# Attention with a gated output: the output projection over pairs of token tiles, and other places for the weight loads

## The chip, the cores and the metric

The kernel runs on one core of a Trainium2 chip. The metric is the device time of one execution in microseconds. Three runs of the kernel before took 563.62, 563.86 and 562.90 us; their median is 563.62 us. The execution that was profiled took 563.68 us, and its trace spans 561.8 us from the first instruction to the last. Times of day in this document ("at 212.36 us") count from the start of that span.

## What is computed

The input x has 2048 tokens of width D = 512. The reference, cut to what matters:

```python
xn = layernorm(x)
# A: attention over the last W = 512 rows of a cache; 32 query heads, 8 key/value heads, Dh = 128
q = (xn @ wq)                      # 2048 x 4096, split into 32 heads
p = softmax(q @ k.T * Dh ** -0.5)  # per head: 2048 x 512
s = concat_heads(p @ v) @ wo       # wo is 4096 x 512
# B: a dense MLP of width F = 1792 on the same xn
g = silu(silu(xn @ w1) @ w2)
out = x + s * g
```

Everything is bfloat16 in memory; matmuls accumulate in float32.

## The kernel before, in words

**Tiling.** The tokens are cut into NBLK = 4 blocks of BLK = 512, a block into BLKT = 4 token tiles of P = 128. The main loop (L454) runs over NSTEP = 128 *steps*: step s is head h = s mod 32 of block b = s // 32. All five engines' orders are written out by hand inside `manual_schedule` (L329): on each engine instructions stand in the order in which the Python code emits them, and an engine takes its own in order.

**One step** emits, between them, parts of four heads (L464 to L489):

- the four scores of head s, one token tile each (`score`, L224), each followed by an exponential on ScalarE that also sums the row (L227);
- `normalise` (L235): a reciprocal (L237) and one multiply per token tile (L239) on VectorE. Tiles 0 and 1 of step s are normalised in step s, tiles 2 and 3 at the head of step s + 1;
- `flip(s - 1)` (L245): one DMA transpose of the normalised probabilities p_all into pT, 512 KB from on-chip memory to on-chip memory, issued from SyncE (SP);
- the q projection of head s + 2, four matmuls and a copy (L205, L214);
- the PV product of head s − LAG, LAG = 3, four matmuls (L256) and a copy to `oT` (L261), the head's output transposed: features on partitions, the block's 512 tokens along the row. So pT of step s is wanted in step s + 3.

**Filler.** `pump(n)` puts n single matmuls of other work between these. In block 0 (steps 0 to 31) the filler is the MLP of blocks 1 to 3 (block 0's MLP is done ahead of the loop). From step 32 on it is the output projection of the block before, 128 matmuls per block, four to a step: two after the third score and two after the fourth. I call them *units*, numbered 0 to 127 within a block; unit u falls in the block's step u // 4.

**The output projection** is made by `out_units(b)` (L285). For token tile j the 32 heads add into one PSUM tile `s_ps` (L294), tag "f" with two buffers: `oT` of the head, the tile's 128 columns, is the stationary operand, and the head's 128 x 512 slice of wo the moving one. At head 16 GpSimd issues the load of the tile's x (`x_e`, L303). After head 31 VectorE multiplies with the gate (`sg`, L307) and adds x (L308), and the result is stored (L311), by GpSimd, or by SP for the last block. The order is tile 0 with heads 0 to 31, then tile 1, and so on. The last block's 160 matmuls (tile 3 in two halves) have no step left to hide in and run after the loop (L504 to L512), among the last three PV products.

**Buffers.** `oT` has OT_BUFS = 53 buffers used in turn. `x_e` has two (tags pair4 and pair5), `sg` two (pair2, pair3); these tags belonged to the MLP before.

**wo** is 4 MB in all and takes the room of the MLP's weights when these are done. It comes in pieces, each one DMA on SP: `wo_plan` (L442) gives for a step the pieces (first head, number of heads; 128 KB per head) that are issued at the step's end (L501, L280). The first four pieces, heads 0 to 13, are issued at the ends of steps 27 to 30; the others, heads 14 to 31, at the ends of steps 32 to 36. A unit needs the piece that holds its head.

**Order on the queues.** SP's queue in this stretch holds the flips and the wo pieces alone[...]. GpSimd's queue holds the x_e loads and the stores of blocks 0 to 2.

Of the kernel before, what the change touches and what calls it, by code (L numbers as in the profile page):

```python
# [9 lines left out]
P = 128  # L10
ALU = mybir.AluOpType
ACT = mybir.ActivationFunctionType
ENG = mybir.EngineType
BF16 = mybir.dt.bfloat16
FP32 = mybir.dt.float32

LAG = 3
OT_BUFS = 53
PS_BUFS = {"sc": 4, "q": 1, "o": 1, "f": 2}


# [1 line left out]
def kernel(  # L23
# [12 lines left out]
    nc = tc.nc  # L36
    _B, SQ, D = A_x.shape
    NTOK = _B * SQ
    _, HKV, SK, DH = A_k_cache.shape
    HQ = A_wq.shape[1] // DH  # L40
# [6 lines left out]
    BLKT = 4  # L47
# [6 lines left out]
    x2 = A_x.flatten_outer_dims()  # L54
# [5 lines left out]
    reg = ctx.enter_context(tc.tile_pool(name="reg", bufs=1))  # L60
    work = ctx.enter_context(tc.tile_pool(name="work", bufs=2))
    ps = ctx.enter_context(tc.tile_pool(name="ps", bufs=1, space=bass.MemoryType.PSUM))
# [10 lines left out]
    g_sb = {}  # L73
# [175 lines left out]
    def pv_units(s):  # L249
# [3 lines left out]
        def mm(kc):  # L253
# [5 lines left out]
            if kc == NKC - 1:  # L259
                oT[s] = work.tile([P, BLK], BF16, name="oT", bufs=OT_BUFS)  # L260
                nc.vector.tensor_copy(oT[s], cur["ps"])  # L261
# [6 lines left out]
    def wo_of(h):  # L268
        for lo, n, t in wo_t:
            if lo <= h < lo + n:  # L270
                return t[:, h - lo, :]
        raise KeyError(h)
# [4 lines left out]
    def load_wo(h0, n):  # L277
        for lo, m, t in wo_t:
            if lo <= h0 < lo + m:
# [2 lines left out]
                    A_wo[ds(h0 * DH, n * DH), :].rearrange("(h p) n -> p h n", p=P),  # L282
                )

    def out_units(b):  # L285
        units = []
        cur = {}
        last = b == NBLK - 1

        def mm(j, h, lo, n):  # L290
            t = b * BLKT + j
            if h == 0:
                cur["ps"] = ps.tile([P, n], FP32, name="s_ps", tag="f", bufs=2)
            nc.tensor.matmul(  # L294
                cur["ps"],
                oT[b * HQ + h][:, j * P : (j + 1) * P],
                wo_of(h)[:, lo : lo + n],
                start=(h == 0),
                stop=(h == HQ - 1),
            )  # L300
            if h == HQ // 2 and lo == 0:
                cur["x"] = reg.tile([P, D], BF16, name="x_e", tag=f"pair{4 + j % 2}")
                nc.gpsimd.dma_start(cur["x"], x2[ds(t * P, P), :])  # L303
            if h == HQ - 1:
                xe = cur["x"][:, lo : lo + n]
                sg = reg.tile([P, n], FP32, name="sg", tag=f"pair{2 + (j + lo // 256) % 2}")
                nc.vector.tensor_tensor(out=sg, in0=cur["ps"], in1=g_sb[b][:, j, lo : lo + n], op=ALU.mult)  # L307
                nc.vector.scalar_tensor_tensor(  # L308
                    out=xe, in0=sg, scalar=0.25, in1=xe, op0=ALU.mult, op1=ALU.add
                )  # L310
                (nc.sync if last else nc.gpsimd).dma_start(out2[ds(t * P, P), lo : lo + n], xe)  # L311

        for j in range(BLKT):
            parts = [(0, D // 2), (D // 2, D // 2)] if last and j == BLKT - 1 else [(0, D)]
            for lo, n in parts:
                for h in range(HQ):
                    units.append(lambda j=j, h=h, lo=lo, n=n: mm(j, h, lo, n))
        return units

    w1v = B_w1.rearrange("(c p) f -> p c f", p=P)  # L320
    w2v = B_w2.rearrange("(c p) d -> p c d", p=P)
# [7 lines left out]
    with tc.manual_schedule(engines={ENG.PE, ENG.Activation, ENG.DVE, ENG.SP, ENG.Pool}):  # L329
# [71 lines left out]
        for i, u in enumerate(hs[NEARLY * ND :]):  # L401
            u()
            f, c = divmod(i + NEARLY * ND, ND)
            if c == ND - 1 and f in (5, 7, 9, 11):
                stats(1, (f - 5) // 2)
        for i, u in enumerate(os_):
# [6 lines left out]
            if i % 4 == 3 and 1 <= i // 4 <= 2 * BLKT:  # L413
                b, j = divmod(i // 4 - 1, BLKT)
# [20 lines left out]
        def pump(n):  # L435
# [8 lines left out]
            HQ - 4: [(4, 3)],  # L444
            HQ - 3: [(7, 4)],
            HQ - 2: [(11, 3)],
            HQ: [(14, 4)],
            HQ + 1: [(18, 3)],
            HQ + 2: [(21, 4)],
            HQ + 3: [(25, 3)],  # L450
            HQ + 4: [(28, 2), (30, 2)],
        }
        wo_first = False
        for s in range(NSTEP):  # L454
            b, h = divmod(s, HQ)
            if b >= 1 and h == 0:
                assert done >= n_mlp or b > 1
                fill += out_units(b - 1)
            n = (h + 1) * n_mlp // HQ - done if b == 0 else 4
# [41 lines left out]
            for args in wo_plan.get(s, []):  # L501
                load_wo(*args)

        fill += out_units(NBLK - 1)  # L504
        s = NSTEP
        normalise(s - 1, 2, 3)
# [36 lines left out]
```

The softmax here doesn't subtract the row's maximum and nothing guards it: scores larger than these inputs give would overflow.

## Time and profile before

| What | Value |
|---|---|
| median of three runs | 563.62 us |
| span of the profiled run | 561.8 us |
| TensorE busy | 549.1 us, 2576 matmuls |
| VectorE busy | 439.7 us |
| ScalarE busy | 385.5 us |
| mean DMA throughput | 160 GB/s |
| DMA transposes pT<-p_all | 128, median 3.7 us from issue to landing |
| granted TensorE clock | 1.00 |

How to read it: TensorE is busy for all but 12.7 us of the span. The page names each group of instructions by line, engine and operation, with out<-in by the program's tile names; "PE" is TensorE's matmuls, "PEld" its weight loads, "SPq" the queue of SyncE, which issues DMAs. In a timeline a row is: start, duration (both us), engine, line, operation, tiles, count, and in brackets the idle time of the engine ahead of it with what ended it. A list of stretches gives for each its length, then busy time of PE, PEld, DVE, ACT and POOL with instruction counts in parentheses, then the granted clock, the mean busy share of the 16 DMA engines, and GB/s; the share counts overlapping packets, so it can exceed 1. In the list of waits a row is: who waited for whom, total us, number of waits, longest.

### The profile page before, as it was taken

What the parts mean: (1) busy time and instruction counts of PE and PEld (TensorE: products, weight loads), DVE (VectorE), ACT (ScalarE), POOL (GpSimd) and SP (SyncE); (2) the same over time, 40 slices, a digit from 0 to 9 for tenths busy, and PEclk for the clock granted to TensorE, in tenths of its full rate; (3) what the DMA queues carried; (4) which work ended last, traced back from release to release, by engine and by line L of the source; (5) the groups of instructions that cost most, each with busy time, mean ns of one, the idle gap of its engine ahead of it and who ended that gap; (6) DMA issues with size and microseconds to landing.
All of it is one profiled execution on the core that took longest, in us unless ns stands there. A gap on an engine that the chain in (4) does not pass through costs nothing.

```text
span 561.8 us, 8230 instructions
## 1 busy us (share of the span) xinstructions
PE 549.1 (98%) x2576; PEld 250.8 (45%) x2576; DVE 439.7 (78%) x1185; ACT 385.5 (69%) x1110; POOL 16.5 (3%) x35
## 2 busy tenths in 40 slices
PE   8989999999999997999999999999999999999997
PEld 4434444444444443444444444444444444444345
DVE  5978877976887685888888888888888888888622
ACT  4758757766776675777777777777777777777400
POOL 0000000000000000000000000000000000000100
PEclk9999999999999999999999999999999999999999
DMA  9638596885747899768676767676868685868701
GB/s 301 177 85 169 115 200 145 158 194 127 169 109 183 161 221 231 169 156 169 151 169 152 168 151 169 151 175 147 182 143 185 137 192 130 191 138 181 179 28 29
DMA packets 297467, 89.67 MB, mean 160 GB/s; under 512 B 282320, under 2 KB 296528, under 8 KB 297424
## 3 DMA queue, kind: packets, MB, share of 16 engines
q1 hardware_dynamic: 295280, 84.83, 67.8%
q0 software_dynamic: 1344, 3.67, 2.8%
q10 hardware_dynamic: 800, 0.66, 0.4%
q8 instruction: 20, 0.33, 0.3%
q14 instruction: 23, 0.19, 0.1%
HBM read 17.30 MB, written 2.10 MB: 35 GB/s over the span
## 4 chain that ended last, share of the span: by engine, by line
PE 87%; DVE 6%; DMA 4%; ACT 2%; issue 1%; ACTq 0%; SPq 0%
PE o_ps L256 19%; PE q_ps L205 19%; PE sc_ps L224 19%; PE s_ps L294 18%; PE oB_ps L172 7%; PE h_ps L138 6%; DMA pT<-p_all 4%; DVE st L104 2%; ACT th L149 1%; DMA x_116<-in_A_x_dram 1%; DVE mv L105 1%; ACT p_all L227 0%; DVE p_all L239 0%; DVE x_122 L115 0%; DVE hT_2_479 L150 0%
## 5 line engine op out<-in xcount | busy, mean ns | idle before, releaser
L227 ACT ACTIVATE p_all<-sc_ps 128x512 bf16<-128x512 f32 x512 | 304.9, 597 | 109.9 <-PE sc_ps L224 100.6
L239 DVE TENSOR_SCALAR p_all<-p_all,rden 128x512 bf16<-128x512 bf16 x512 | 157.8, 350 | 9.1
L261 DVE CAST oT<-o_ps 128x512 bf16<-128x512 f32 x128 | 88.2, 689 | 51.7 <-PE o_ps L256 51.6
L227 ACT ACTIVATION_READ_ACCUMULATOR p_all<-sc_ps 128x1 f32 x512 | 100.6, 196 | 0.0
L214 DVE CAST qT<-q_ps 128x512 bf16<-128x512 f32 x128 | 88.0, 687 | 2.8 <-PE q_ps L205 2.8
L294 PEld LDWEIGHTS <-oT 128*128 128x128 bf16 x544 | 53.2, 98 | 57.6
L224 PEld LDWEIGHTS <-qT 128*128 128x128 bf16 x512 | 50.1, 98 | 61.6 <-issue 1.8
L237 DVE RECIPROCAL rden<-den 128x2 f32<-128x2 f32 x256 | 40.6, 159 | 14.5 <-ACT p_all L227 14.5
L149 ACT ACTIVATE th<-h_ps 128x512 bf16<-128x512 f32 x56 | 33.4, 598 | 10.6 <-PE h_ps L138 8.4
L294 PE MATMUL s_ps<-wo_2010,oT 128*128 128x512 bf16 (+1 forms) x119 | 33.0, 366 | 0.0
L294 PE MATMUL s_ps<-wo_2317,oT 128*128 128x512 bf16 (+1 forms) x119 | 33.0, 366 | 0.0
L294 PE MATMUL s_ps<-wo_2318,oT 128*128 128x512 bf16 (+1 forms) x119 | 32.8, 367 | 0.0
L294 PE MATMUL s_ps<-wo_2011,oT 128*128 128x512 bf16 (+1 forms) x119 | 32.8, 367 | 0.0
L224 PE MATMUL sc_ps<-kT_89,qT 128*128 128x512 bf16 x64 | 24.3, 379 | 0.0
L224 PE MATMUL sc_ps<-kT_91,qT 128*128 128x512 bf16 x64 | 24.3, 379 | 0.0
L224 PE MATMUL sc_ps<-kT_86,qT 128*128 128x512 bf16 x64 | 24.3, 379 | 0.0
L224 PE MATMUL sc_ps<-kT_87,qT 128*128 128x512 bf16 x64 | 24.3, 379 | 0.0
L224 PE MATMUL sc_ps<-kT_90,qT 128*128 128x512 bf16 x64 | 24.3, 379 | 0.0
L224 PE MATMUL sc_ps<-kT_88,qT 128*128 128x512 bf16 x64 | 24.3, 379 | 0.0
L224 PE MATMUL sc_ps<-kT_85,qT 128*128 128x512 bf16 x64 | 24.3, 379 | 0.0
L224 PE MATMUL sc_ps<-kT_92,qT 128*128 128x512 bf16 x64 | 23.9, 379 | 0.0
L256 PE MATMUL o_ps<-pT,v_94 128*128 128x512 bf16 x64 | 17.1, 379 | 1.9 <-DMA pT<-p_all 1.9
(198 smaller groups left out, 700.0 us busy)
## 6 DMA issues: line engine op xcount, KB each, us to landing
pT<-p_all SPq DMA_TRANSPOSE x128, 3.7
x_e<-in_A_x_dram POOLq DMA_DIRECT2D x16, 128.0 KB, 2.9
out_dram<-x_e POOLq DMA_DIRECT2D x12, 128.0 KB, 2.2
w_1_106<-in_B_w_dram SPq DMA_DIRECT2D x1, 896.0 KB, 8.1
w_0_107<-in_B_w_dram SPq DMA_DIRECT2D x1, 896.0 KB, 11.2
w_1_108<-in_B_w_dram SPq DMA_DIRECT2D x1, 896.0 KB, 13.2
w_0_105<-in_B_w_dram SPq DMA_DIRECT2D x1, 512.0 KB, 5.6
x_122<-in_A_x_dram SPq DMA_DIRECT2D x1, 512.0 KB, 9.1
```

The costliest lines, as they stand in the source:

```text
L138: nc.tensor.matmul(h_ps[:, lo : lo + n], w1_sb[f // FH][:, c, (f % FH) * P : (f % FH + 1) * P], xnT[b][:, c, lo : lo + n], start=(c == 0), ...
L149: nc.scalar.activation(th, h_ps, ACT.Tanh, scale=0.5)
L172: nc.tensor.matmul(cur["ps"], hT[b][f // 2][:, f % 2, j * P : (j + 1) * P], w2_sb[f // FH][:, f % FH, :], start=(f == 0), stop=(f == NFC - 1),
L205: nc.tensor.matmul(cur["ps"], wq_sb[h // REP][:, c, (h % REP) * DH : (h % REP + 1) * DH], xnT[b][:, c, :], start=(c == 0), stop=(c == ND - 1),
L214: nc.vector.tensor_copy(qT[s], cur["ps"])
L224: nc.tensor.matmul(sc, qT[s][:, j * P : (j + 1) * P], kT[h // REP], start=True, stop=True)
L227: nc.scalar.activation(p_all[s][:, :, j, :], sc.rearrange("p (kc q) -> p kc q", q=P), ACT.Exp, scale=INV_SQRT_DH, accum_out=den[s][:, j : ...
L237: nc.vector.reciprocal(rden, den[s][:, j0 : j1 + 1])
L239: nc.vector.tensor_scalar_mul(p_all[s][:, :, j, :], p_all[s][:, :, j, :], rden[:, j - j0 : j - j0 + 1])
L256: nc.tensor.matmul(cur["ps"], v_sb[h // REP][:, kc, :], pT[s][:, kc, :], start=(kc == 0), stop=(kc == NKC - 1))
L261: nc.vector.tensor_copy(oT[s], cur["ps"])
L294: nc.tensor.matmul(cur["ps"], oT[b * HQ + h][:, j * P : (j + 1) * P], wo_of(h)[:, lo : lo + n], start=(h == 0), stop=(h == HQ - 1),)
```

## The change

Three things are edited.

1. The order of the units of blocks 0 to 2. A new function `out_order` walks through two token tiles j0 and j0 + 1 at a time: two heads of j0, then two heads of j0 + 1, eight heads (LEAD) behind. The last block keeps its order. Tile j0 now starts at unit 0 and ends at unit 53, tile j0 + 1 starts at unit 10 and ends at unit 63; the second pair likewise from 64 on (64 to 117 and 74 to 127). The matmuls of a block are the same 128. Two accumulations are now open at once, one in each of the two "f" buffers, so the dictionary that held one PSUM tile and one x_e holds one for each j.
2. The wo pieces for heads 14 to 31 go from the ends of steps 32 to 36 to the ends of steps 33, 35, 37, 39 and 41. In the new order, head 14 is first wanted by unit 20 (step 37), head 18 by unit 28 (step 39), head 21 by unit 33 (step 40), head 25 by unit 41 (step 42) and head 28 by unit 48 (step 44). Before, they were wanted in steps 35, 36, 37, 38 and 39.
3. `oT` gets 48 buffers instead of 53. A head's output is last read by the fourth tile, which starts at unit 74 instead of 96.

On GpSimd's queue the order load, store, load, store of a block's x_e and results becomes load, load, store, store for each pair.

```diff
-OT_BUFS = 53
+OT_BUFS = 48
+LEAD = 8
...
+    def out_order(last):
+        order = []
+        for j0 in range(0, BLKT, 2):
+            if last:
+                for j in (j0, j0 + 1):
+                    parts = [(0, D // 2), (D // 2, D // 2)] if j == BLKT - 1 else [(0, D)]
+                    order += [(j, h, lo, n) for lo, n in parts for h in range(HQ)]
+                continue
+            for h in range(0, HQ + LEAD, 2):
+                if h < HQ:
+                    order += [(j0, h, 0, D), (j0, h + 1, 0, D)]
+                if h >= LEAD:
+                    order += [(j0 + 1, h - LEAD, 0, D), (j0 + 1, h - LEAD + 1, 0, D)]
+        return order
+
     def out_units(b):
-        units = []
-        cur = {}
+        acc = {}
+        xes = {}
         last = b == NBLK - 1
 
         def mm(j, h, lo, n):
             t = b * BLKT + j
             if h == 0:
-                cur["ps"] = ps.tile([P, n], FP32, name="s_ps", tag="f", bufs=2)
+                acc[j] = ps.tile([P, n], FP32, name="s_ps", tag="f", bufs=2)
             nc.tensor.matmul(
-                cur["ps"],
+                acc[j],
...
             if h == HQ // 2 and lo == 0:
-                cur["x"] = reg.tile([P, D], BF16, name="x_e", tag=f"pair{4 + j % 2}")
-                nc.gpsimd.dma_start(cur["x"], x2[ds(t * P, P), :])
+                xes[j] = reg.tile([P, D], BF16, name="x_e", tag=f"pair{4 + j % 2}")
+                nc.gpsimd.dma_start(xes[j], x2[ds(t * P, P), :])
...
-        for j in range(BLKT):
-            parts = [(0, D // 2), (D // 2, D // 2)] if last and j == BLKT - 1 else [(0, D)]
-            for lo, n in parts:
-                for h in range(HQ):
-                    units.append(lambda j=j, h=h, lo=lo, n=n: mm(j, h, lo, n))
-        return units
+        return [lambda a=a: mm(*a) for a in out_order(last)]
...
-            HQ: [(14, 4)],
-            HQ + 1: [(18, 3)],
-            HQ + 2: [(21, 4)],
-            HQ + 3: [(25, 3)],
-            HQ + 4: [(28, 2), (30, 2)],
+            HQ + 1: [(14, 4)],
+            HQ + 3: [(18, 3)],
+            HQ + 5: [(21, 4)],
+            HQ + 7: [(25, 3)],
+            HQ + 9: [(28, 2), (30, 2)],
```

More of the change, by code (lines that the diff above doesn't have):

```diff
@@ L301, in mm @@
             if h == HQ // 2 and lo == 0:
-                cur["x"] = reg.tile([P, D], BF16, name="x_e", tag=f"pair{4 + j % 2}")
-                nc.gpsimd.dma_start(cur["x"], x2[ds(t * P, P), :])
+                xes[j] = reg.tile([P, D], BF16, name="x_e", tag=f"pair{4 + j % 2}")
+                nc.gpsimd.dma_start(xes[j], x2[ds(t * P, P), :])
             if h == HQ - 1:
-                xe = cur["x"][:, lo : lo + n]
+                xe = xes[j][:, lo : lo + n]
                 sg = reg.tile([P, n], FP32, name="sg", tag=f"pair{2 + (j + lo // 256) % 2}")
-                nc.vector.tensor_tensor(out=sg, in0=cur["ps"], in1=g_sb[b][:, j, lo : lo + n], op=ALU.mult)
+                nc.vector.tensor_tensor(out=sg, in0=acc[j], in1=g_sb[b][:, j, lo : lo + n], op=ALU.mult)
                 nc.vector.scalar_tensor_tensor(
```

## The prediction

> **What bounds the kernel now.** The page's first part comes first: is there an engine with nothing left to give?
>
> ```profile
> span 561.8 us, 8230 instructions
> ...
> PE 549.1 (98%) x2576; PEld 250.8 (45%) x2576; DVE 439.7 (78%) x1185; ACT 385.5 (69%) x1110; POOL 16.5 (3%) x35
> ```
>
> TensorE is busy for 549.1 of 561.8 us, and the change neither adds nor removes a matmul. Only the 12.7 us between them can be won, and each of the gaps has to be found. The list of PE's waits has one large entry, the chain of waits places it, and PE's timeline between 195 and 230 us shows it:
>
> ```profile
> PE o_ps L256 <- DMA pT<-p_all: 4.2, 5, 1.9
> ```
>
> ```profile
> 205.74 16.30 DMA pT<-p_all x3
> ```
>
> ```profile
> 207.52 1.03 PE L256 MATMUL o_ps<-pT,v_93 128*128 128x512 bf16 x4
> ...
> 212.36 1.04 PE L256 MATMUL o_ps<-pT,v_93 128*128 128x512 bf16 x4 [1.22 <-DMA pT<-p_all]
> ...
> 216.56 1.04 PE L256 MATMUL o_ps<-pT,v_93 128*128 128x512 bf16 x4 [0.57 <-DMA pT<-p_all]
> ...
> 222.08 1.04 PE L256 MATMUL o_ps<-pT,v_94 128*128 128x512 bf16 x4 [1.89 <-DMA pT<-p_all]
> ...
> 225.54 1.03 PE L256 MATMUL o_ps<-pT,v_94 128*128 128x512 bf16 x4
> ```
>
> Each row is the PV product (`o_ps`) of one step. A step after block 0 has 16 matmuls and takes 3.455 us wherever nothing waits (from 315.44 to 343.07 us, eight of them take 27.63). From 207.52 to 225.54 us four steps take 18.02 instead of 13.82: **4.2 us are lost here**, all of it waiting for the transposed probabilities (pT) of steps 34, 35 and 36. (The brackets add to 3.7; a matmul's modelled end laps over the next start, so I count from row to row.) Outside this place and the last steps the trace has PV rows 3.455 us apart to the end of block 3, but for a single 0.1 us at 260 us.
>
> Why they are late is in SyncE's own timeline and in the DMA share of a busy and a quiet stretch of equal length:
>
> ```profile
> 201.13 0.58 SPq L280 DMA_DIRECT2D wo_2317<-in_A_wo_dram  x1
> 201.87 3.08 SPq L245 DMA_TRANSPOSE pT<-p_all  x1
> 204.99 0.58 SPq L280 DMA_DIRECT2D wo_2318<-in_A_wo_dram  x1
> 205.74 4.58 SPq L245 DMA_TRANSPOSE pT<-p_all  x1
> 210.37 0.58 SPq L280 DMA_DIRECT2D wo_2318<-in_A_wo_dram  x1
> ```
>
> ```profile
> 195.00:222.00 27.00, 23.39 (x107) 10.12 (x105) 19.93 (x57) 17.11 (x52) 0.00 (x0) 1.00 1.03 212
> 315.00:342.00 27.00, 27.00 (x127) 12.22 (x126) 23.06 (x65) 20.73 (x63) 1.08 (x2) 1.00 0.71 159
> ```
>
> The last two columns are DMA share and GB/s. In the quiet stretch a transpose holds SP for 1.3 to 2.3 us and lands 3.7 us after issue (median). In the crowded one it holds SP for up to 4.58 us and lands after 5.0 to 6.6; the engines are at 1.03. By the packets, a transpose costs 2.31 us of all 16 engines (18.47 us for eight), and the 2.30 MB of later wo cost 8.78 us, 0.49 us per head of 128 KB. Five consecutive steps that carry 4, 3, 4, 3 and 4 heads need 5 × 2.31 + 18 × 0.49 = 20.3 us in 17.3. The slack of pT (landing to first use) shows the debt growing: 3.15 us in quiet steps, 0.9 for step 32, 0.45 for 33, then the three stalls.
>
> **What the Trainium skill says.** "DMA: Bandwidth & Descriptors", Issuing engines are not separate DMA queues: transfers started by any engine share the same 16 DMA engines. The trace agrees: where GpSimd's store and load stand beside a transpose, it lands after 4.8 us instead of 3.65. The same page, Latency and other measured facts, gives 261 GB/s for a strided DMA transpose; this trace has 512 KB in 2.31 us, 227 GB/s, which I use. "TensorE: Matmul & The Clock Gate", Wait — 56ns, not 53.3ns?, gives 215.7 ns between matmuls of 512 columns; here 3.455/16 = 0.216 us, with the granted clock at 1.00. "PSUM — Partial Sum Buffer", The four PSUM rules: two open accumulations disturb each other only in one bank; the two s_ps tiles have a bank each, as they did before.
>
> **The change part by part.**
>
> 1. *The later wo pieces move* from the ends of steps 32, 33, 34, 35, 36 to 33, 35, 37, 39, 41. Six DMA issues move, of 0.47 to 0.58 us on SP each, past one to five transposes; nothing else is in SP's queue there, and GpSimd's is not touched by this. Two steps now need 2 × 2.31 + 4 × 0.49 = 6.6 us in 6.91 for the large pieces and 6.1 for the small ones: 95% and 88%. It fits, narrowly. The first piece goes out when pT 32 has been issued (197.5 + 1.6 = 199.1 us); if its 1.95 us all came ahead of pT 33 (ready at 200.6), that would land near 206.1, 1.4 us ahead of its use at 207.5; pT 34 has a step to itself and lands near 208.5 to 209.2 for use at 210.98. The debt is paid every other step. Value: **−4.2 us**; ends 0 and −4.2.
> 2. *Two token tiles side by side* are 128 matmuls per block as before, in another order. Rows of sc_ps, s_ps, q_ps and o_ps already alternate between banks 0.216 us apart, so the order costs TensorE nothing. It is what lets the pieces come later: head 14 is first wanted in step 37 instead of 35, then head 18 in 39, 21 in 40, 25 in 42, 28 in 44. With the longest landing of such a piece here (5.5 us) they arrive 4.2 to 7 us early. No wait. With step 29's 6.9 us they still would.
> 3. *The evacuations move.* sg and x_e (L307, L308; 1.33 us of VectorE from start to next start) for a block's four tiles stood at the ends of steps 7, 15, 23, 31; now they stand in the middle of 13, at the end of 15, in the middle of 29, at the end of 31. Each delays one normalise: pT slack falls to 0.97 us and is back at 3.2 two steps later, which is just the new distance; nothing is lost. The places in 39 and 55 become quieter.
> 4. *At the end* the steps 126 and 127 lack the q product (12 matmuls, 2.59 us) and VectorE is nearly full, so the tile that now ends in step 125 instead of 119 matters. I inserted 1.33 us after the normalise at 521.05 us and walked VectorE's rows forward:
>
> ```profile
> 521.84 0.17 DVE L237 RECIPROCAL rden<-den 128x2 f32<-128x2 f32 x1 [0.17 <-ACT p_all L227]
> ...
> 522.84 0.69 DVE L261 CAST oT<-o_ps 128x512 bf16<-128x512 f32 x1 [0.19 <-PE o_ps L256]
> ```
>
> The brackets are idle time, waiting for ScalarE and PE, that the later rows take up. The transpose of step 125 goes out 0.8 us later, 126's 0.5, and 127's, on which the final PV waits, 0.2 (529.19 instead of 528.96). Value **+0.2**; ends 0 and +1.1 (hardly any idle time taken up).
> 5. *Stores and loads.* GpSimd's order was load, store, load, store; it becomes two loads, two stores. After the second store of a pair two x_e loads follow instead of one, just where a pT has 0.97 us of slack. 256 KB beside a transpose cost 1.13 us of landing time (4.78 against 3.65), so 128 KB more cost some 0.57, and 0.4 us of slack remain. Five places (steps 47, 63, 79, 95, 111), of which before one ran down to 0.05 us and one to 0.41. Value **+0.1**; ends 0 and +1. Behind the waiting load stand only stores and loads needed a step or more later.
> 6. *48 head outputs instead of 53.* In step 19 of a block head 16's copy takes the buffer that tile 3's product with head 0 read at the end of step 18, ten matmuls (2.2 us) earlier; the later heads have more. VectorE does not wait: 0.
>
> Sum: −4.2 + 0.2 + 0.1 = −3.9 on the profiled span, 561.8 → 557.9. The profiled run took 563.68 us by the clock that gives the times, 1.9 more than its span, and the other runs are 562.9 to 563.86; off the median of 563.62 it is **559.7 us**, 0.7% less.
>
> **The rivals.**
>
> - *The crowd stays in part.* For it: 95% of the DMA engines with a packet mix that has reached 1.03; single transposes that land after 7.3 us elsewhere (step 5). Against: in steps 27 to 29 pieces of the same size, one to a step of 4.9 us, left most transposes at 3.7. Half of 4.2 stays: 561.8.
> - *The wo pieces are not the cause.* The slack had already fallen to 2.06 at step 31, where the last MLP evacuations make VectorE late; if that debt alone does it, 563.6 to 564. Against: step 32 then starts without a new piece, and its normalise is ready at 197.45, in time.
> - *Slower: paired evacuations turn into a new wait.* The second store and two loads meet the late pT five times. It decides from a landing of 3.65 + 1.13 + 0.97 = 5.75 us on. At 6.8 us each place costs 1 us; with the end's +1.1 and half the crowd, 563.62 − 2.1 + 5 + 1.1 = 567.6. For it: 5.8 us was reached at 254 us. Against: nine of eleven places in the old order stand at 4.8.
>
> **How the numbers follow.** Chances: forecast (558.9 to 560.8) 0.72; part of the crowd stays (560.8 to 562.5) 0.14; within 0.2%, about what a measurement here can tell (562.5 to 564.7), 0.08; slower 0.06. Faster is 0.86. The range is 558.9 to 561.9: below it there is nothing but run-to-run spread (562.9 − 4.2 = 558.7), and above it up to half of the crowd is held.
>
> **What would show it.** Right: PE's wait for pT is under 1 us and no PV row between 200 and 240 us stands more than 3.5 us after the last; the transposes there hold SP for about 2 us and land within 5.4; the wo pieces stand 6.9 us apart; the last PV starts some 0.2 us later than the end of the quiet steps makes it. Wrong: brackets at PV rows near 205 to 230 us (first rival), or the same three brackets (second), or new ones near the steps 47, 63, 79, 95, 111 (third). What would make the sum wrong without any of these is a matmul pitch other than 0.216 us.

## The result and the profile after

The changed kernel took 559.83, 559.82, 559.62 and 559.91 us, median **559.83 us**, beside 563.74 us for the kernel before in the same comparison: ratio 0.9925, 95% interval 0.9898 to 0.9952. The forecast was 559.7. In the kernel's file the lines are shifted: what was L205, L224, L256, L294, L307 is now L206, L225, L257, L312, L325.

The page's first lines, after:

```profile
span 557.7 us, 8232 instructions
...
PE 548.2 (98%) x2576; PEld 251.2 (45%) x2576; DVE 439.9 (79%) x1185; ACT 386.2 (69%) x1110; POOL 16.6 (3%) x35
```

The work is the same and the span is 4.1 us shorter. From the list of PE's waits, the entry that had 4.2 us in five places:

```profile
PE o_ps L257 <- DMA pT<-p_all: 1.2, 1, 1.2
```

The PV products in PE's timeline where the three stops were, with no bracket left and 3.45 us from row to row:

```profile
207.50 1.03 PE L257 MATMUL o_ps<-pT,v_93 128*128 128x512 bf16 x4
...
210.95 1.03 PE L257 MATMUL o_ps<-pT,v_93 128*128 128x512 bf16 x4
...
214.41 1.03 PE L257 MATMUL o_ps<-pT,v_93 128*128 128x512 bf16 x4
...
217.86 1.03 PE L257 MATMUL o_ps<-pT,v_94 128*128 128x512 bf16 x4
```

From the PV row of step 29 to that of step 44 the kernel before took 56.01 us, this one 51.80: **4.21 us**. SyncE's timeline there, and the DMA share of the stretch that stood at 1.03 (last two columns: share and GB/s):

```profile
199.14 0.57 SPq L281 DMA_DIRECT2D wo_2317<-in_A_wo_dram  x1
200.67 5.11 SPq L246 DMA_TRANSPOSE pT<-p_all  x2
205.83 0.58 SPq L281 DMA_DIRECT2D wo_2317<-in_A_wo_dram  x1
207.58 5.04 SPq L246 DMA_TRANSPOSE pT<-p_all  x2
212.66 0.58 SPq L281 DMA_DIRECT2D wo_2318<-in_A_wo_dram  x1
```

```profile
195.00:222.00 27.00, 27.00 (x127) 12.23 (x126) 22.75 (x65) 21.13 (x63) 0.00 (x0) 1.00 0.96 218
```

Two transposes now stand between two pieces (a merged row runs from the first's start to the second's end). From step 33 to 44 each holds SP for 1.3 to 3.0 us, and pT's slack stays between 1.7 and 3.2 us from step 32 to 44.

The end of the loop pays a little back, as forecast. VectorE's rows where tile 2 of block 2 now ends, and the PV product that waits for it:

```profile
517.24 0.69 DVE L325 TENSOR_TENSOR sg<-s_ps,gate_1403 128x512 f32<-128x512 f32 x1
517.96 0.69 DVE L326 SCALAR_TENSOR_TENSOR x_e<-sg,x_e 128x512 bf16<-128x512 f32 x1
518.57 0.16 DVE L238 RECIPROCAL rden<-den 128x2 f32<-128x2 f32 x1
```

```profile
523.55 1.04 PE L257 MATMUL o_ps<-pT,v_100 128*128 128x512 bf16 x4 [1.21 <-DMA pT<-p_all]
```

At the last three PV products, one wait of 1.37 us (row to row) and one of 0.13 replace the three of 0.43; from the PV row of step 122 to that of step 127 it is 14.88 us instead of 14.66. The balance: −4.21, +0.22, and −0.10 for a wait at step 47 that is gone, −4.1 in all.

### The profile page after: what moved, and what is told of

The parts are those of the page before. It is cut to its first block, busy times and chain, and to the rows that moved or that the text cites. A ratio compares the mean times of both kernels' runs of the same rounds, so it can differ in the third digit from the quotient of the medians.

```text
span 557.7 us, 8232 instructions
## 1 busy us (share of the span) xinstructions
PE 548.2 (98%) x2576; PEld 251.2 (45%) x2576; DVE 439.9 (79%) x1185; ACT 386.2 (69%) x1110; POOL 16.6 (3%) x35
## 4 chain that ended last, share of the span: by engine, by line
PE 91%; DVE 5%; ACT 2%; DMA 1%; issue 1%; ACTq 0%
PE o_ps L257 20%; PE s_ps L312 20%; PE q_ps L206 19%; PE sc_ps L225 19%; PE oB_ps L173 7%; PE h_ps L139 6%; DVE st L105 2%; ACT th L150 1%; DMA pT<-p_all 1%; DMA x_116<-in_A_x_dram 1%; DVE mv L106 1%; ACT p_all L228 0%; DVE x_122 L116 0%; DVE hT_2_479 L151 0%; DVE hT_2_185 L151 0%
## 5 line engine op out<-in xcount | busy, mean ns | idle before, releaser
L312 PEld LDWEIGHTS <-oT 128*128 128x128 bf16 x544 | 53.2, 98 | 57.6
L225 PEld LDWEIGHTS <-qT 128*128 128x128 bf16 x512 | 50.1, 98 | 61.6 <-issue 1.8
L312 PE MATMUL s_ps<-wo_2010,oT 128*128 128x512 bf16 (+1 forms) x119 | 33.0, 366 | 0.0
L312 PE MATMUL s_ps<-wo_2317,oT 128*128 128x512 bf16 (+1 forms) x119 | 33.0, 366 | 0.0
L312 PE MATMUL s_ps<-wo_2318,oT 128*128 128x512 bf16 (+1 forms) x119 | 32.8, 366 | 0.0
L312 PE MATMUL s_ps<-wo_2011,oT 128*128 128x512 bf16 (+1 forms) x119 | 32.8, 366 | 0.0
L225 PE MATMUL sc_ps<-kT_86,qT 128*128 128x512 bf16 x64 | 24.3, 379 | 0.0
L225 PE MATMUL sc_ps<-kT_87,qT 128*128 128x512 bf16 x64 | 24.3, 379 | 0.0
L225 PE MATMUL sc_ps<-kT_89,qT 128*128 128x512 bf16 x64 | 24.3, 379 | 0.0
L225 PE MATMUL sc_ps<-kT_91,qT 128*128 128x512 bf16 x64 | 24.3, 379 | 0.0
L225 PE MATMUL sc_ps<-kT_90,qT 128*128 128x512 bf16 x64 | 24.3, 379 | 0.0
L225 PE MATMUL sc_ps<-kT_85,qT 128*128 128x512 bf16 x64 | 24.2, 379 | 0.0
L225 PE MATMUL sc_ps<-kT_88,qT 128*128 128x512 bf16 x64 | 24.2, 379 | 0.0
L225 PE MATMUL sc_ps<-kT_92,qT 128*128 128x512 bf16 x64 | 23.9, 379 | 0.0
L139 PEld LDWEIGHTS <-w_0_105 128*128 128x128 bf16 x128 | 12.3, 98 | 13.2 <-issue 1.5
```

The lines of the kernel that those rows point to most:

```text
L139: nc.tensor.matmul(h_ps[:, lo : lo + n], w1_sb[f // FH][:, c, (f % FH) * P : (f % FH + 1) * P], xnT[b][:, c, lo : lo + n], start=(c == 0), ...
L225: nc.tensor.matmul(sc, qT[s][:, j * P : (j + 1) * P], kT[h // REP], start=True, stop=True)
L312: nc.tensor.matmul(acc[j], oT[b * HQ + h][:, j * P : (j + 1) * P], wo_of(h)[:, lo : lo + n], start=(h == 0), stop=(h == HQ - 1),)
```

## Experiments

Each is compared with the kernel before on the same chip, which took 563.1 to 563.7 us (medians).

**e1: the new order of units with the old places of the pieces.**

```diff
-            HQ + 1: [(14, 4)],
-            HQ + 3: [(18, 3)],
-            HQ + 5: [(21, 4)],
-            HQ + 7: [(25, 3)],
-            HQ + 9: [(28, 2), (30, 2)],
+            HQ: [(14, 4)],
+            HQ + 1: [(18, 3)],
+            HQ + 2: [(21, 4)],
+            HQ + 3: [(25, 3)],
+            HQ + 4: [(28, 2), (30, 2)],
```

> The changed kernel with the later wo pieces back at the ends of steps 32 to 36; order of units and 48 buffers stay. Theory (the crowd of wo pieces is the cause, the new order of units alone gives nothing): TensorE again stops at the PV products of steps 34 to 36 for about 4.2 us in all, pT slack there falls to 0.05 us, and the time is 559.8 + 4.2 = 564.0. Rival (the gain comes from the new order of units, for example from the VectorE work of tile 0 that leaves step 39): no stop, about 559.8.

Measured: 564.02 us, ratio 0.9998 (0.9986 to 1.0010). The stops of steps 34 to 36 are back, 3.9 us in all from row to row; PE's timeline shows the first and the last:

```profile
212.10 1.04 PE L257 MATMUL o_ps<-pT,v 128*128 128x512 bf16 x4 [0.82 <-DMA pT<-p_all]
...
221.91 1.82 PE L257 MATMUL o_ps<-pT,v 128*128 128x512 bf16 x4 [1.99 <-DMA pT<-p_all]
```

The new order by itself gives nothing and costs nothing; the places of the pieces make the difference.

**e3: one pair only.** The side-by-side order for tiles 0 and 1 of block 0, everything else in the old order, 53 buffers.

```diff
-OT_BUFS = 48
+OT_BUFS = 53
...
-            if last:
+            if b > 0 or j0 > 0:
+                last = b == NBLK - 1
```

> The changed kernel with the side-by-side order for the first two tiles of block 0 alone, all other tiles in the old order, and 53 buffers again. Theory: the whole gain comes from the time that this one pair buys for the wo pieces; no stop in steps 34 to 36; the last PV products of steps 122 to 127 take 14.66 us again instead of 14.88, as no evacuation falls into step 125. About 559.6. Rival (the other pairs or the buffers have a share in the gain): above 560.5.

Measured: 559.69 us, ratio 0.9930 (0.9915 to 0.9944), no stop in steps 34 to 36, and 1.24 us of waiting at the last three PV products. So one of the six pairs carries the whole gain, and neither the other pairs nor the number of buffers has a share that can be seen.

**e5: no later pieces at all.**

```diff
     def wo_of(h):
+        h = h % 14
...
-            HQ: [(14, 4)],
-            HQ + 1: [(18, 3)],
-            HQ + 2: [(21, 4)],
-            HQ + 3: [(25, 3)],
-            HQ + 4: [(28, 2), (30, 2)],
```

> The kernel before without the loads of wo for heads 14 to 31; those heads' products use the slices of heads 0 to 13 instead, so the projection is another one, with the same instructions on every engine but SyncE. Theory (the later wo pieces alone make the transposes late): no stop of TensorE between 200 and 240 us, 563.7 - 4.2 = 559.5, and a small spread from run to run. Rival (a debt from the end of block 0, visible in the slack of 2.06 us at step 31, is what lets steps 34 to 36 run late): part of the stops stays, above 561.

Measured: 559.93 us (two runs, 559.87 and 559.98), ratio 0.9945 (0.9927 to 0.9963). No stop; the slack of pT, 2.1 at step 31, is 2.85 in step 32 and 3.15 in step 33. The low value at step 31 heals in two steps; it is no cause.

**e6 and e8: how much per step.** The changed kernel with two heads of wo in each of nine steps (e6) or three in each of six (e8).

```diff
-            HQ + 1: [(14, 4)],
-            HQ + 3: [(18, 3)],
...
+            **{HQ + 1 + i: [(14 + 2 * i, 2)] for i in range(3)},
+            HQ + 4: [(20, 1), (21, 1)],
+            **{HQ + 5 + i: [(22 + 2 * i, 2)] for i in range(5)},
```

> The changed kernel with the later wo as nine pieces of two heads at the ends of nine consecutive steps, 33 to 41, instead of five pieces in every other step. Theory (what counts is work per time on the DMA engines: 2.31 + 0.98 = 3.29 us in 3.455): no stop, pT slack about level around 2 us, 559.8. Rival (a pause of one step after each piece is needed): the slack falls from step to step and TensorE stops before step 41, above 561.

> The changed kernel with three heads of wo at the ends of six consecutive steps, 33 to 38. Theory (debt): 2.31 + 1.47 = 3.78 us of DMA work in 3.455, so the slack of pT falls by about 0.3 us per step from 2.9 and stands near 1 us after six: no stop, 559.8. With four heads to a step, as in every other step of the kernel before, the fall is 0.8. Rival (above full load everything queues and late transposes delay one another): slack reaches 0.05 and TensorE stops, 561 or more.

Measured: e6 560.77 us, ratio 0.9954 (0.9929 to 0.9978), slack 2.2 to 3.2 us from step 33 to 41, no stop; e8 560.37 us, 0.9953 (0.9935 to 0.9971), with one first, small stop. PE's timeline of e8:

```profile
214.41 1.03 PE L257 MATMUL o_ps<-pT,v 128*128 128x512 bf16 x4
...
218.03 1.04 PE L257 MATMUL o_ps<-pT,v 128*128 128x512 bf16 x4
```

These rows are 3.62 us apart, 0.16 over a step. The slack in steps 32 to 39 was 2.9, 2.6, 1.5, 2.1, 0.05, 0.8, 0.3, 1.6: downwards, but in jumps and further than the 0.3 us per step that I had worked out. Two heads per step fit, three just do, 3.6 (e1) stop TensorE for 3.9 us. And the number of pieces in SyncE's queue is not it: e6 has one or two in every step. The rest of e6 and e8 over the changed kernel is not in this stretch; 0.5 and 0.6 us of it are longer waits at the last PV products, and in e6 another 0.25 us lies behind the last of them. Why the same order waits longer there in these two runs is open.

**e2 and e9: other queues for the pieces.** The kernel before, later pieces issued by GpSimd (e2) or by ScalarE (e9).

```diff
-                nc.sync.dma_start(
+                (nc.gpsimd if h0 >= 14 else nc.sync).dma_start(
```

> The kernel before with the later wo pieces issued by GpSimd at the same steps instead of SyncE. Theory (the 16 DMA engines have more work in these five steps than time, 20.3 us in 17.3): the stops stay, 3 to 4.5 us in all, about 563.6. Rival (the pieces do harm because they stand in SyncE's queue between the transposes and hold them up there): transposes are issued as soon as their data is there, land in about 4.5 us, no stop, about 559.5.

> The kernel before with the later wo pieces issued by ScalarE at the ends of the same steps instead of SyncE, so that no transpose stands behind a piece in SyncE's queue, and the pieces keep their places in time (which GpSimd, running ahead, did not). Theory (the DMA engines have too much work in these steps, whoever issues it): transposes of steps 32 to 36 still land 5 us or more after issue, TensorE still loses 3 us or more between 200 and 225 us; 563 or more, as ScalarE also pays for the issues. Rival (the pieces harm by holding the transposes up in SyncE's queue): they are issued when their data is ready, land within 4.8 us, and no wait of PV products for pT is left; 561 or less.

Measured: e2 **572.85 us**, ratio 1.0164 (1.0149 to 1.0180). This run answers another question than I asked: GpSimd has nothing else to do and issued all six pieces between 189.85 and 195.7 us. Two stretches of e2 (columns as in the lists of stretches above: the last three are granted clock, DMA share, GB/s):

```profile
195.00:201.00 6.00, 5.76 (x27) 2.44 (x25) 5.53 (x17) 4.02 (x12) 1.35 (x2) 1.00 1.12 276
205.00:211.00 6.00, 0.00 (x0) 0.00 (x0) 0.00 (x0) 0.00 (x0) 0.00 (x0) 0.50 1.28 87
```

TensorE did not run a matmul in the second one, the transpose of step 31 landed 16 us after its issue, and the transfers moved 87 GB/s at a DMA share of 1.28.

e9 leaves the pieces at the ends of their steps and is the cleaner test, and my theory lost it: **560.47 us**, ratio 0.9938 (0.9901 to 0.9975). Three tenths of a microsecond of waiting remain between 195 and 225 us (0.26 at step 31, 0.06 at step 35), against 4.2. The same stretch, before TensorE's first stop, in the kernel before and in e9:

```profile
196.50:210.00 13.50, 13.50 (x64) 6.17 (x63) 11.36 (x33) 10.34 (x32) 0.00 (x0) 1.00 1.07 225
```

```profile
196.50:210.00 13.50, 13.35 (x62) 5.96 (x62) 11.10 (x33) 10.04 (x31) 0.00 (x0) 1.00 1.18 268
```

The 16 engines moved 225 GB/s when transposes and pieces came through SyncE's queue alone, and 268 when they came through two. The engines were not at their limit before. The transposes of steps 32 to 38, in the kernel before and in e9 (how long they held SP in ns, minimum, median and maximum, with the first and the last issue; then from issue to landing):

```profile
L245 SPq DMA_TRANSPOSE pT<-p_all x7: 1641/3077/4584, 197.5 to 221.9; - x7
DMA to landing us min/median/max: 3.8/5.4/6.6
```

```profile
L245 SPq DMA_TRANSPOSE pT<-p_all x7: 1317/2706/3237, 197.7 to 218.5; - x7
DMA to landing us min/median/max: 3.8/5.4/6.8
```

From issue to landing they took as long as before, not the 4.8 us at most that the rival had named. What changed is when they went out: that of step 34, the first to stop TensorE, at 204.59 instead of 205.74 us, and the last of the seven 3.4 us earlier, in part because the stops themselves are gone. So the pieces slow a transpose from either queue (without them, in e5, it lands after 3.6 to 3.8 us), and e9 runs close, with a slack of 0.05 us at steps 31 and 35; what stops TensorE is that on SyncE's queue they also make the transposes go out late. Of e9's 0.6 us over the changed kernel, 0.3 are in this stretch and about 0.4 at the last PV products.

**e4, e7, e11: filling the end.** The changed kernel with units ahead of the last three PV products (e4), and e3 with the same, two units shifted (e7).

```diff
-        for i, n in enumerate((6, 14, 0)):
+        for i, n in enumerate((8, 6, 14)):
+            pump(n)
             for u in pv_units(s - LAG + i):
                 u()
-            pump(n)
```

> The changed kernel with the 28 units after the loop placed as 8, 6 and 14 AHEAD of the last three PV products, instead of 6, 14 and 0 after them. In the changed kernel TensorE stands idle for 1.36 us ahead of the PV product of step 125 and 0.12 ahead of that of step 127. Theory: the units fill this wait and nothing else waits longer: 559.8 - 1.5 = 558.3. Rival (the last transpose or a copy of the head outputs moves later by as much): 559.8.

> One pair side by side (as e3), with 8, 6 and 12 units ahead of the last three PV products. In e4 the product with head 31 of the last block's first tile still waits 0.3 us for the last head output, as three units stand between; now five do. Theory: no wait of TensorE after step 32 over 0.2 us; 559.7 - 1.0 (what e3 still waits at the end: 0.68 + 0.18 + 0.38 = 1.2, less a rest) = 558.5 or a little less, equal to or below e4. Rival (the last transpose, not the units, sets the start of the last PV product): 559 or more.

Measured: e4 558.67 us, ratio 0.9912 (0.9897 to 0.9927); the waits ahead of the PV products are gone, and the unit of head 31 starts 0.30 us late, at the copy of the last head output. e7 (8, 6, 12) 558.67 us, ratio 0.9920 (0.9907 to 0.9934). Every wait of PE's matmuls in e7:

```profile
PE q_ps L206 <- DVE qT L215: 1.6, 1, 1.6
PE warm_ps L365 <- POOL warm L338: 1.5, 1, 1.5
PE t_ps L370 <- DVE x L116: 1.2, 1, 1.2
PE h_ps L139 <- ACT rstd L109: 0.6, 1, 0.6
PE h_ps L139 <- DVE hT L151: 0.3, 1, 0.3
```

All of these lie before 50 us, in the start and the change from the first MLP to the loop. As e4, e7 and the changed kernel had run on different chips, I ran them once more side by side, with e9 given the same end:

> The changed kernel, unaltered, on the chip of the two that follow. 559.8; waits only ahead of the last PV products, about 1.5 us.

> e7 (one pair side by side, 8, 6 and 12 units ahead of the last three PV products) on the same chip. 1.0 to 1.6 us below the changed kernel, 558.3 to 558.8. Rival (the difference lay between the chips): within 0.5 us of it.

> The order of tiles before, later wo pieces issued by ScalarE at the old steps (as e9), and the tail of e7. If SyncE's queue was what made the transposes late, no side-by-side order is needed: 560.5 - 1.8 (the two waits at the end of e9) + 0.3 at most = 558.7 to 559.0. Rival (e9's result was chance, its slack of 0.05 turns into waits of 1 us or more): 559.7 or more.

Measured: the changed kernel 559.80 us (559.79 to 560.24), ratio 0.9933 (0.9917 to 0.9950); one pair with the filled end **558.72 us** (558.58 to 558.85), 0.9912 (0.9896 to 0.9928); pieces by ScalarE with the filled end 559.27 us (559.02 to 559.68), 0.9924 (0.9905 to 0.9944). The second is the best version that I found. The third comes without the side-by-side order, 0.5 us behind, and still waits 0.40 us at step 31 and 0.52 at the end, a little more than I had allowed.

## Why the prediction was right, and where its reason was not

**The pieces (−4.2).** The size was right, 4.21. The two landings worked out were close: pT of step 33 at 206.1 forecast, 205.3 measured; of step 34 at 208.5 to 209.2, measured 208.65. The reason was wrong in one step: "Five consecutive steps … need … 20.3 us in 17.3" took the sum of packet times as the share of the 16 engines that is used up. In e9 the same bytes passed at a share of 1.18 with 0.3 us of waiting. Packet times overlap, so a share near 1 was no ceiling here. The section of the Trainium skill that the prediction draws on ("DMA: Bandwidth & Descriptors", Issuing engines are not separate DMA queues) also says that issuing from several engines saves only the issuing sequencer's time, usually small beside the transfer. Here it was not small: with the pieces on ScalarE's queue 3.9 of the 4.2 us of waiting went, and the GB/s of the stretch rose too.

What had no room left is SyncE's queue. SP takes one instruction after the other, and these rows, with those in the prediction, leave no pause of more than 0.2 us:

```profile
197.51 3.57 SPq L245 DMA_TRANSPOSE pT<-p_all  x1
...
211.06 3.39 SPq L245 DMA_TRANSPOSE pT<-p_all  x1
214.50 0.58 SPq L280 DMA_DIRECT2D wo_2319<-in_A_wo_dram  x1
215.12 0.47 SPq L280 DMA_DIRECT2D wo_2320<-in_A_wo_dram  x1
```

From 197.5 to 218.5 us five transposes (the fifth from 215.75, 2.79 us) held SP for 17.4 us and five pieces for 2.8, 20.2 in all, with 17.3 us to do it in. The same five transposes held it for 7.7 us without pieces (e5) and for 12.2 with the pieces on ScalarE's queue (e9). A transpose right behind a piece held SP for 2.8 to 4.6 us instead of the 1.3 to 1.7 of most quiet steps. In the changed kernel every second transpose follows another transpose, and the others have a pause of about 1 us ahead of them: they held it for 1.3 to 3.0. Why SP is held longer behind a piece no run here tells. The size of this term was read from the trace and owed nothing to the wrong reason; that the new places were wide enough was luck in part, because both readings ask for the same remedy, fewer bytes of wo per step. In e8 the packet sum promised a slack that falls by 0.3 us per step and no stop, and was wrong. (A slip without effect: 18 × 128 KB of wo are 2.36 MB, not 2.30.)

**Two tiles side by side (0).** Right: e1, ratio 0.9998. No product waited for a piece.

**Evacuations (0).** Right: slack 2.06 at step 45 (evacuation in the middle of 13) and 0.98 at step 47, with no wait.

**The end (+0.2).** Right, 0.22. The transposes of steps 125, 126 and 127 went out 1.06, 0.53 and 0.24 us later against the end of the quiet steps; forecast were 0.8, 0.5 and 0.2. In other runs of the same order this place cost up to 0.6 us more (e6, e8). One sign named for being right did not come: TensorE's wait for pT was to be under 1 us and is 1.2, all of it at step 125.

**Stores and loads (+0.1).** Too pessimistic, 0. I had the second x_e load beside the late transpose. It first has to wait for the store of its own buffer to land, as GpSimd's timeline shows:

```profile
249.59 0.55 POOL L329 DMA_DIRECT2D out_dram<-x_e  x1 [6.36 <-DVE rden L238]
250.13 0.54 POOL L321 DMA_DIRECT2D x_e<-in_A_x_dram  x1
252.01 0.54 POOL L321 DMA_DIRECT2D x_e<-in_A_x_dram  x1 [1.34 <-DMA out_dram<-x_e]
```

That wait makes it the neighbour of the next transpose, which has slack to give (2.3 us instead of 2.6). The slack at the five places is 0.91 to 1.01 us; before it was 0.93 to 1.00, and 0.05 at step 47. (The 0.41 us that the prediction counts among the five stood at step 87, which is none of them.) The margin is not safe: in e6 and e8, with the same order of loads, the slack at step 63 was 0.18 and 0.26 us, still without a wait.

**48 buffers (0).** Right: no copy to `oT` waits for a product of the projection, and e3, with 53, takes the same time.

**The sum (559.7).** That it came within 0.13 us is luck in part: the span fell by 4.1 us instead of 3.9, and the time beyond the span was 2.1 us instead of the 1.9 taken over from before.

**The rivals.** That the pieces are not the cause falls with e5 and e1. The slower case fell with the profile after. The first rival, part of the crowd stays, did not come true, but its ground did: three heads per step are already at the edge (e8).

## What to carry to other kernels

Look at the queue that issues before you add up what the DMA engines do: a queue without a pause between its instructions was the bound here while the DMA engines could still do more, and a bulk load put between urgent transfers lengthened the time that the next one held the queue. Either spread the bulk over more steps, as the change does, or give it another in-order queue that keeps its time; a queue that runs ahead can send the whole bulk at once, which was the worst of all here (e2). And where the last product of a pipeline waits for its last transfer, put independent work ahead of the wait instead of after it (worth about 1.1 us: e4, and e11 beside e10).

## What the runs showed that I had not expected

The gain has a second part that a single profile does not hold. The kernel before scatters (25 runs beside e1 to e8: 562.4 to 565.9 us), the changed kernel hardly does (eight runs: 559.6 to 560.2). In the profiled run of e1 the last stop of 2.16 us was followed by 3.4 us at half the TensorE clock, matmuls 0.43 us apart:

```profile
222.50:226.00 3.50, 3.50 (x11) 1.28 (x10) 1.38 (x4) 1.94 (x8) 0.00 (x0) 0.58 0.87 197
```

Of those 25 runs the four slowest (564.7, 565.5, 565.7, 565.9) are the ones with a mean granted clock of 0.997; all others have 0.999 or 1.000. Of the 12 runs beside e9 to e12 the two slowest (564.8, 565.8) are again those with 0.997. 0.3% of 562 us is the 1.7 us that half speed for 3.4 us costs. The rest of the scatter, up to 564.6 us at a full clock, is not explained by this. The Trainium skill ("TensorE: Matmul & The Clock Gate", What's actually happening) has the clock halved after an idle window of about 3.4 us; in this run a stop of 2.2 us with two shorter ones in the 12 us ahead was enough. That the other runs with 0.997 had the same is inferred from their mean clock and time.
